# Projection of k and v of the batch after next in one block with the values of a head pair, in an attention and feed-forward kernel

## Chip, core and metric

The kernel runs on one core of a Trainium2 chip. The metric is the device time of one execution in microseconds (us). Engines are named as in the profile: PE is the matrix engine (TensorE), PEld its weight loads, DVE the vector engine, ACT the scalar engine, POOL the engine whose queue issues the input loads, SP the engine whose queue issues stores and small copies.

## What is computed

Eight batches of linear attention (keys and values of 1024 positions are projected to 64), eight heads of 64, followed by a feed-forward layer with a squared rectifier:

```python
k_proj = einsum('ks,bhsd->bhkd', E, k)          # E, F: 64 x 1024
v_proj = einsum('ks,bhsd->bhkd', F, v)
scores = q @ k_proj.T / sqrt(64)
attn   = softmax(scores, axis=-1)
x      = (attn @ v_proj)  -> rows (b, s), columns (h, d): 8192 x 512
h      = maximum(x @ w_in, 0)                   # w_in 512 x 2048
out    = (h * h) @ w_out                        # w_out 2048 x 512
```

Output is float32; the kernel computes in bf16 with float32 accumulation.

## The kernel before, in words

**Feed-forward.** A batch's tokens are two chunks of 512. Both products of the feed-forward layer are done, from batch 1 on, as block products with seven partial products in place of eight. The first product of a chunk runs in four *groups* (class `Group`), the second in `second_spread`. A generator `both()` takes one *step* at a time: one stage of a group (four matmuls of 128x256, line 680) and then one piece of the second product of the chunk before (line 594). A group takes seven steps, in the order of `F_STEPS`: p1, p5, p4 of the group before, p6, p2, p3, p7. A chunk takes 28 steps, a batch 56.

**Banks.** [...] `psum` holds four single banks (`bank0` to `bank3`) for the first product and a pair (`att_psum`) for attention; `second_pool` holds two for the second product. In a group, `first` is bank base+1, `other` is base+2, and `chain` is base+3 for an even group and base+4 (the same as base+0) for an odd one. After p2 a group has no more use for `first`, and the chain bank of the other parity is free from p4 to the next p1. Values of a head pair can therefore be computed into these two banks between p3 and the next p1: `values_lent`. DVE then has to empty them (`scale`, line 421, two instructions of 128x512) before the next group's p1 writes `first` (line 707) and ACT copies `first` to `chain` (line 708).

**Attention of the next batches** is put between the steps by a plan: `on(step, b, name, ...)` calls a method of `atts[b]` after that step. For loop index b the count starts at t = 56(b-1)+28, the middle of batch b's first products. In the 28 steps after t the attention of batch b+1 is finished; then follow the projection, transposes and scores of b+2. The methods are

- `scores(pr)`: two matmuls (line 339), exponentials on ACT (line 353), `att_psum`
- `sums_spread(pr)`: sums of two pairs (eight matmuls of 64x32 tiles, line 392), logarithm and exponential on ACT (lines 396, 397), then six SP copies that spread the inverse sums `rs` (line 403); `rs` has three buffers
- `values_products` / `scale`: four matmuls of 64x64 tiles (line 413) and the two DVE multiplications by `rs` into xT (line 421)
- `project`: sixteen matmuls, k and v in turn in tiles of 128x64 (lines 270, 271) into `att_psum`, then k twice into `kp` on DVE (lines 258, 259) and v into `vp` once on ACT (line 263) and once on DVE (line 264)
- `transpose_q_dma`, `transpose_k_dma`: SP transposes (lines 331, 304)
- `load_q`, `load_kv`: POOL loads, each held behind a named earlier instruction: `load_q` behind the last instruction that `atts[b+1].done` names when the plan reaches it, `load_kv` behind the transpose of k

**Order.** PE runs in the order written. On DVE, ACT and SP a scheduler fixes the order when the program is built, and each engine then runs its own list in order. One rule ties DVE to a lent bank: after a `values_lent`, the `relu_sum` of that group's p7 (line 697) is placed after its `scale`. In `Group`, p3 and p7 end in a `relu_sum` on DVE, p2 and p4 in a rectifier on ACT (line 690); in odd groups DVE then squares h (128x1024) and forms four sums (`sum_h`), all line 154.

Of the kernel before, what the change touches and what calls it, by code (L numbers as in the profile page):

```python
# [19 lines left out]
def kernel(  # L20
# [46 lines left out]
    turn = {"att": 0, "bank": 0, "step": 1, "pairs": 2}  # L67

    lent = ctx.enter_context(ExitStack())
# [5 lines left out]
    def att_psum(shape=(P, 2, TCH), dtype=F32):  # L75
        turn["att"] += 1
        return pair_psum(turn["att"] % turn["pairs"], shape, dtype)

    def bank(shape=(P, 512), dtype=F32, n=None):
        if n is None:  # L80
            turn["bank"] += turn["step"]
            n = turn["bank"]
        return psum.tile(list(shape), dtype, tag=f"bank{n % 4}", name="ps_bank")
# [48 lines left out]
    for j, (lo, hi) in enumerate(W_IN_PIECES):  # L132
        t = wpool.tile([P, NCB, (hi - lo) * P], BF16, name=f"w_in_{lo}")
# [7 lines left out]
    for j in range(WP):  # L141
        t = wpool.tile([P, fn, DM], BF16, name=f"w_out_{j}")
# [89 lines left out]
    class Attention:  # L232
# [170 lines left out]
                            nc.sync.dma_start(rs[j][to:to + 32], rs[0][have:have + 32])  # L403
                self.rs[pr + j] = rs[j]

        def values_products(self, pr, lent):
            ps_x = [bank(n=turn["bank"] + n)[:] for n in (1, 4)] if lent else None
            if not lent:
                ps = att_psum()
                ps_x = [ps[:, par] for par in range(2)]  # L410
            e = self.e.pop(pr)
            for o, par, a, r in VALUE_QUADS:
                nc.tensor.matmul(  # L413
                    ps_x[par][o], lhsT=self.vp[r, 2 * pr + a, :], rhs=e[r, a], start=True, stop=True
                )
            self.ps_x[pr] = ps_x
# [8 lines left out]
            return self.done  # L425

        def values(self, pr):
            self.values_products(pr, False)
            self.scale(pr)

        def values_lent(self, pr):
            self.values_products(pr, True)
            turn["lent"] = self.scale(pr)


# [303 lines left out]
    with tc.manual_schedule(engines={PE}):  # L739
# [33 lines left out]
        def at(step, fn, *args, **kwargs):  # L773
            plan.setdefault(step, []).append(lambda: fn(*args, **kwargs))
# [110 lines left out]
        def on(step, b, name, *args):  # L885
            at(step, lambda: getattr(atts[b], name)(*args))
# [5 lines left out]
        for b in range(B - 1):  # L892
            t = 56 * (b - 1) + 28
            if b:
                on(t + 1, b + 1, "scores", 3)
                on(t + 6, b + 1, "sums_spread", 2)
                on(t + 6, b + 1, "values_lent", 1)
                on(t + 10, b + 1, "values", 0)
                on(t + 20, b + 1, "values_lent", 2)
                on(t + 20, b + 1, "values_products", 3, False)  # L900
                on(t + 21, b + 1, "scale", 3)
                at(t + 24, lambda b=b: chunk[b + 1, 0].sum_x())
            at(t + 51, lambda b=b: chunk[b + 1, 1].sum_x())
            if b + 2 < B:
                if b:
                    on(t + 11, b + 2, "load_q", lambda b=b: atts[b + 1].done)
                on(t + (26 if b else 32), b + 2, "transpose_q_dma")
                on(t + (28 if b else 36), b + 2, "project")
                on(t + (30 if b else 37), b + 2, "transpose_k_dma")
                if b + 3 < B:  # L910
                    at(t + (32 if b else 37), begin, b + 3)
                    on(t + (32 if b else 37), b + 3, "load_kv", lambda b=b: atts[b + 2].kT_done)
                on(t + (44 if b else 45), b + 2, "scores", 0)
                on(t + (47 if b else 48), b + 2, "scores", 1)
                on(t + (50 if b else 51), b + 2, "sums_spread", 0)
                on(t + (53 if b else 54), b + 2, "scores", 2)
# [34 lines left out]
```

## Time and profile before

| | us |
|---|---|
| three runs | 471.1, 471.76, 474.29; median 471.76 |
| the profiled execution | 472.65, of which the span from first to last instruction is 470.9 |
| PE busy | 464.3 (99%), 4141 matmuls |
| PEld busy | 369.2 (78%) |
| DVE busy | 347.1 (74%), 596 instructions |
| ACT busy | 298.3 (63%) |
| POOL busy | 34.2 (7%) |
| granted PE clock | 0.996 |
| DMA | 64.75 MB, mean 138 GB/s |

Busy shares are means over the whole span; matmuls overlap in the pipe, so a busy PE is not one at its peak. A timeline row gives the start in us from the beginning of the span, the duration, engine, line, operation, output<-input, shape and how many equal instructions follow each other; in square brackets stands the idle time ahead of it and what ended that.

### The profile page before, as it was taken

What the parts mean: (1) busy time and instruction counts of PE and PEld (TensorE: products, weight loads), DVE (VectorE), ACT (ScalarE), POOL (GpSimd) and SP (SyncE); (2) the same over time, 40 slices, a digit from 0 to 9 for tenths busy, and PEclk for the clock granted to TensorE, in tenths of its full rate; (3) what the DMA queues carried; (4) which work ended last, traced back from release to release, by engine and by line L of the source; (5) the groups of instructions that cost most, each with busy time, mean ns of one, the idle gap of its engine ahead of it and who ended that gap; (6) DMA issues with size and microseconds to landing.
All of it is one profiled execution on the core that took longest, in us unless ns stands there. A gap on an engine that the chain in (4) does not pass through costs nothing.

```text
span 470.9 us, 10084 instructions
## 1 busy us (share of the span) xinstructions
PE 464.3 (99%) x4141; PEld 369.2 (78%) x4141; DVE 347.1 (74%) x596; ACT 298.3 (63%) x484; POOL 34.2 (7%) x47
## 2 busy tenths in 40 slices
PE   7999999999999999999999999999999999999997
PEld 3544587788888887888888888888878888888886
DVE  2468976776977779677895679777796778968571
ACT  3568777777556873688556775568736885565641
POOL 7340010100010000100001000100000000000000
PEclk8999999999999999999999999999999999999999
DMA  9999999795949577594868749495682042101012
GB/s 182 201 205 207 158 161 198 161 217 158 170 102 183 153 135 179 103 173 127 163 169 141 163 132 163 114 194 138 135 180 69 27 126 74 68 24 68 24 70 89
DMA packets 84592, 64.75 MB, mean 138 GB/s; under 512 B 33985, under 2 KB 81857, under 8 KB 84545
## 3 DMA queue, kind: packets, MB, share of 16 engines
q0 software_dynamic: 32208, 29.23, 40.4%
q1 hardware_dynamic: 52336, 34.88, 27.6%
q8 instruction: 32, 0.52, 0.5%
q14 instruction: 16, 0.12, 0.1%
HBM read 59.24 MB, written 16.78 MB: 161 GB/s over the span
## 4 chain that ended last, share of the span: by engine, by line
PE 96%; DMA 1%; ACT 1%; DVE 0%; SPq 0%; issue 0%; DVEq 0%
PE ps_bank L680 37%; PE ps_second L594 36%; PE ps_bank L513 6%; PE ps_bank L573 3%; PE ps_att L339 3%; PE ps_att L270 3%; PE ps_second L573 1%; DMA k_f<-in_k_dram 1%; PE ps_bank L413 1%; PE ps_att L392 1%; PE ps_att L413 1%; PE ps_bank L220 1%; PE ps_bank L314 1%; ACT rs L358 1%; PE ps_bank L278 1%; PE ps_att L349 0%
## 5 line engine op out<-in xcount | busy, mean ns | idle before, releaser
L154 DVE TENSOR_TENSOR h<-h 128x1024 bf16<-128x1024 bf16 (+1 forms) x170 | 105.4, 645 | 43.8 <-ACT h L690 38.6
L680 PEld LDWEIGHTS <-w_in_sum 128*128 128x128 bf16 x896 | 85.4, 98 | 20.0 <-issue 7.4
L680 PE MATMUL ps_bank<-x_sum,w_in_sum 128*128 128x256 bf16 x672 | 101.1, 273 | 0.0
L594 PEld LDWEIGHTS <-h 128*128 128x128 bf16 x896 | 87.7, 98 | 10.3
L697 DVE CUSTOM_DVE_ANT_0 h<-ps_bank,u 128x512 bf16<-128x512 f32 x112 | 74.2, 685 | 14.0 <-PE ps_bank L680 9.7
L708 ACT COPY ps_bank<-ps_bank 128x512 f32<-128x512 f32 x56 | 32.0, 571 | 82.7 <-PE ps_bank L680 82.4
L568 ACT COPY u<-ps_bank 128x512 f32<-128x512 f32 x115 | 68.0, 591 | 22.6 <-PE ps_bank L680 20.9
L690 ACT ACTIVATE h<-ps_bank 128x512 bf16<-128x512 f32 x112 | 67.9, 606 | 14.0 <-PE ps_bank L680 13.1
L680 PEld LDWEIGHTS <-w_in 128*128 128x128 bf16 x672 | 65.3, 98 | 12.1 <-issue 2.5
L594 PEld LDWEIGHTS <-s 128*128 128x128 bf16 x672 | 65.7, 98 | 7.7
L680 PE MATMUL ps_bank<-xT,w_in 128*128 128x256 bf16 x448 | 67.3, 273 | 0.0
L594 PE MATMUL ps_second<-w_out_sum,s 128*128 128x256 bf16 x448 | 67.2, 273 | 0.0
L594 PE MATMUL ps_second<-w_out_sum,h 128*128 128x256 bf16 x448 | 67.0, 273 | 0.0
L594 PE MATMUL ps_second<-w_out,h 128*128 128x256 bf16 x448 | 64.7, 272 | 0.0
L353 ACT ACTIVATE expT<-ps_att 128x1024 bf16<-128x1024 f32 x32 | 33.1, 1034 | 5.6 <-PE ps_att L339 5.3
L154 DVE TENSOR_TENSOR o_sb<-ps_second,u 128x512 f32<-128x512 f32 x29 | 19.8, 684 | 19.3 <-PE ps_second L594 13.6
L680 PE MATMUL ps_bank<-xT,w_in_sum 128*128 128x256 bf16 x224 | 33.6, 273 | 0.0
L680 PE MATMUL ps_bank<-x_sum,w_in 128*128 128x256 bf16 x224 | 33.6, 273 | 0.0
L594 PE MATMUL ps_second<-w_out,s 128*128 128x256 bf16 x224 | 33.6, 273 | 0.0
L513 PE MATMUL ps_bank<-xT,w_in 128*128 128x512 bf16 x128 | 29.1, 379 | 0.0
L421 DVE TENSOR_TENSOR xT<-ps_att,rs 128x512 bf16<-128x512 f32 x24 | 15.4, 682 | 14.9 <-PE ps_att L413 14.9
L568 ACT COPY u<-ps_second 128x512 f32<-128x512 f32 x30 | 17.6, 585 | 11.6 <-PE ps_second L594 9.3
(98 smaller groups left out, 478.7 us busy)
## 6 DMA issues: line engine op xcount, KB each, us to landing
out_dram<-o_sb SPq DMA_DIRECT2D x63, 256.0 KB, 2.4
rs<-rs SPq DMA_DIRECT2D x72, 128.0 KB, 2.3
K_sb<-in_k_dram POOLq DMA_DIRECT2D x7, 1024.0 KB, 10.0
V_sb<-in_v_dram POOLq DMA_DIRECT2D x7, 1024.0 KB, 14.6
Q_sb<-in_q_dram POOLq DMA_DIRECT2D x6, 1024.0 KB, 9.2
w_out<-in_moe_w_out_dram POOLq DMA_DIRECT2D x4, 512.0 KB, 16.3
Q_sb<-in_q_dram POOLq DMA_DIRECT2D x4, 256.0 KB, 11.0
V_sb<-in_v_dram POOLq DMA_DIRECT2D x2, 512.0 KB, 10.7
```

The source lines that it names most:

```text
L154: return nc.vector.tensor_tensor(out=o, in0=x, in1=y, op=op)
L270: nc.tensor.matmul(ps[LO, 0], lhsT=ET[:, i, :], rhs=self.K[:, :, i, :], start=f, stop=l)
L353: self.done = nc.scalar.activation(e[:], ps[:], AF.Exp, scale=SCALE)
L421: self.done = nc.vector.tensor_tensor(out=self.xT[:, pr, :, par], in0=ps_x[par].rearrange("p (c t) -> p c t", c=2), in1=rs[:, par].rearran ...
L513: nc.tensor.matmul(ps[:], lhsT=w_in_blk(cb, fb), rhs=self.xT[:, cb, self.c].rearrange("p a t -> p (a t)"), start=(cb == 0), stop=(cb == NC ...
L568: nc.scalar.copy(u[:], ps)
L573: nc.tensor.matmul(ps[:, i * HM:(i + 1) * HM], lhsT=self.h_form(n, fb)[:, i * P:(i + 1) * P], rhs=w_out_form(n, fb), start=fresh and fb == ...
L594: nc.tensor.matmul(ps[:, i * HM:(i + 1) * HM], lhsT=self.h_form(n, fb)[:, i * P:(i + 1) * P], rhs=w_out_form(n, fb), start=fresh and i == ...
L680: nc.tensor.matmul(ps[:, j * HC:(j + 1) * HC], lhsT=w_in_form(n, cb, 2 * self.g + j), rhs=self.chunk.x_form(n, cb), start=fresh and j == 0 ...
L690: nc.scalar.activation(self.out(kh, a), ps[:], AF.Relu)
L697: nc.vector._custom_dve(TENSOR_ADD_SAT, out=self.out(kh, a), in0=ps[:], in1=more[:], s0=3.0e38, s1=0.0)
L708: nc.scalar.copy(self.chain[:], self.first[:])
```

## The change

For loop index b of 1 and above, the values of pair 0 are no longer computed at step t+10 into `att_psum` but at t+13 into lent banks, after p3 of the second group (an odd one, hence the other chain bank: the argument `group`). The projection of batch b+2 (b from 1 to 5) is no longer called at t+28 but at t+13 too, right after these values, into `att_psum`. The other calls keep their steps.

```diff
-        def values_products(self, pr, lent):
-            ps_x = [bank(n=turn["bank"] + n)[:] for n in (1, 4)] if lent else None
+        def values_products(self, pr, lent=0):
+            ps_x = [bank(n=turn["bank"] + n)[:] for n in (1, 4 - lent % 2)] if lent else None
...
         def values(self, pr):
-            self.values_products(pr, False)
+            self.values_products(pr)
             self.scale(pr)
 
-        def values_lent(self, pr):
-            self.values_products(pr, True)
+        def values_lent(self, pr, group):
+            self.values_products(pr, 2 + group)
             turn["lent"] = self.scale(pr)
...
                 on(t + 1, b + 1, "scores", 3)
                 on(t + 6, b + 1, "sums_spread", 2)
-                on(t + 6, b + 1, "values_lent", 1)
-                on(t + 10, b + 1, "values", 0)
-                on(t + 20, b + 1, "values_lent", 2)
-                on(t + 20, b + 1, "values_products", 3, False)
+                on(t + 6, b + 1, "values_lent", 1, 0)
+                on(t + 13, b + 1, "values_lent", 0, 1)
+                on(t + 20, b + 1, "values_lent", 2, 2)
+                on(t + 20, b + 1, "values_products", 3)
                 on(t + 21, b + 1, "scale", 3)
...
                 if b:
                     on(t + 11, b + 2, "load_q", lambda b=b: atts[b + 1].done)
                 on(t + (26 if b else 32), b + 2, "transpose_q_dma")
-                on(t + (28 if b else 36), b + 2, "project")
+                on(t + (13 if b else 36), b + 2, "project")
                 on(t + (30 if b else 37), b + 2, "transpose_k_dma")
```

## The prediction, made before the changed kernel ran

> **What bounds the kernel now.** I read busy shares first, then what PE waited for, then the chain of waits through one batch, then the timelines of PE, DVE and ACT around the moved steps. The busy line and the waits of PE (engine, line, waited for: us, times, longest):
>
> ```profile
> PE 464.3 (99%) x4141; PEld 369.2 (78%) x4141; DVE 347.1 (74%) x596; ACT 298.3 (63%) x484; POOL 34.2 (7%) x47
> ```
>
> ```profile
> PE ps_bank L220 <- DVE zeros L123: 1.2, 1, 1.2
> PE ps_bank L278 <- ACT K_sb L742: 1.0, 1, 1.0
> PE ps_bank L211 <- DVE e_bf L741: 0.7, 1, 0.7
> PE ps_att L339 <- DVE kT L301: 0.2, 1, 0.2
> ```
>
> These four are all, and all belong to the start-up: from 95 to 400 us PE waits for nothing. Its order sets the end, so a change gains only by making PE's own list cheaper, and loses whatever new wait it puts there. What the list costs is in the chain, here in batch 2 (start, length, what):
>
> ```profile
> 164.10 0.34 PE ps_att L392 x8
> 164.44 0.34 PE ps_bank L413 x4
> 164.78 0.54 PE ps_bank L680 x4
> ...
> 168.81 0.34 PE ps_att L413 x4
> 169.15 0.54 PE ps_bank L680 x4
> 169.70 0.44 PE ps_second L594 x4
> ...
> 177.99 0.34 PE ps_bank L413 x4
> 178.33 0.22 PE ps_att L413 x4
> 178.55 0.54 PE ps_bank L680 x4
> ```
>
> Four 128x256 matmuls cost 0.44, but 0.54 straight after a block in smaller tiles; four quads cost 0.22 after quads of the same tile, 0.34 after another tile size. So entering a block costs 0.12 and leaving it 0.10. Sums and then values (64x32, then 64x64) pay the 0.12 twice. `project` enters with 0.33 where its next seven pairs take 0.21 each.
>
> The second resource is DVE, idle 2.5 us ahead of the values of pair 0 and then almost never (start, length):
>
> ```profile
> 169.21 1.29 DVE L421 TENSOR_TENSOR xT<-ps_att,rs 128x512 bf16<-128x512 f32 x2 [2.48 <-PE ps_att L413]
> 171.24 0.69 DVE L154 TENSOR_TENSOR h<-h 128x1024 bf16<-128x1024 bf16 x1 [0.74 <-ACT h L690]
> 171.84 1.28 DVE L697 CUSTOM_DVE_ANT_0 h<-ps_bank,u 128x512 bf16<-128x512 f32 x2
> ...
> 177.80 0.68 DVE L697 CUSTOM_DVE_ANT_0 h<-ps_bank,u 128x512 bf16<-128x512 f32 x1
> 178.40 1.28 DVE L421 TENSOR_TENSOR xT<-ps_bank,rs 128x512 bf16<-128x512 f32 x2
> ```
>
> See that the scale of pair 2 starts at 178.40, its first half ends 178.40+0.68 = 179.08, and p1 of the fourth group, which overwrites that lent bank, starts at 179.37 (PE timeline): a margin of 0.29.
>
> **The Trainium skill.** "TensorEngine Tiling (Array Packing)", Key Properties: changing the tiling mode drains the engine, changing only the tile does not. The trace agrees: 0.12 and 0.10 at each change, 0.22 quads within a mode. "PSUM — Partial Sum Buffer", PSUM bank collisions: the hardware doesn't arbitrate between engines on a bank, semaphores must; hence p1's wait for `scale`. No delay from it shows before. "DMA: Bandwidth & Descriptors", Issuing engines are not separate DMA queues: loads from POOL and copies from SP share 16 engines; used for the loads below. The 128x512 multiplications from PSUM take 0.68 here, which I use instead of any page's price.
>
> **The change on PE.** No matmul is added or removed (the built PE lists have equal length); places change. Removed per batch (b = 1 to 5): the lone values block at t+10, 0.34+0.10 = 0.44, and the lone project block at t+28, 0.33+7x0.21+0.10 = 1.90 with rounding. Added: one block with both. It saves one exit, 0.10, surely. Whether it saves an entry too depends on 64x64 to 128x64: sums to values, the nearest row, pays 0.12 again. I take **-0.10 a batch**, other end -0.22. For b = 6 only the values move: 0.
>
> **The change on DVE.** This is the cost. Moved into the busy stretch at t+13: two scales, two copies to kp, one to vp: five instructions. The built order there is: square, relu_sum p3, scale, square, scale, kp, kp, relu_sum p7, vp, square, sum, square, three sums, then relu_sum p3 and the scale of pair 2 in the next group. From the first square to that scale are 16 starts. Before, ten starts from 171.84 to 178.40 took 6.56, less 0.21 idle: 0.635 each; independent ones come every 0.60, dependent ones every 0.72. Take x = 0 at the start of p3 of the second group (170.84 before). The square, released by ACT, stays at x = 171.24-170.84 = 0.40. Then relu_sum 1.01, scale 1.61 (values are out of PE at 1.4), square 2.21, scale 2.82, kp 3.42 (project, begun near 1.26, ends 1.92 later as before, 3.2), kp 4.02 to 4.70, relu_sum p7 4.62 to 5.30. ACT's vp copy waits for the second kp as in the old lists, so 4.72 to 5.30; DVE's vp 5.35, square 5.95, sum 6.67, square 7.28 (it reads ACT's rectifier of p4, out near 7.0), sums 7.89, 8.50, 9.22, relu_sum p3 9.83, scale of pair 2 at 10.43, first half done **11.11**.
>
> PE on the same clock: p3 and second product to 0.88, values 0.97, project near 1.26, p7 near 3.1. After p7, spacing as before: p4 at +2.62 (six stages of 0.437) = 5.7, p1 of the fourth group at +(179.37-171.72) = 7.65, so **10.75**. DVE is late by 11.11-10.75 = 0.36, with release 0.4. Bounds: at 0.60 a start it is in time, 0; at 0.66, 0.9. I take **+0.4 a batch**. Queued behind the waiting p1 is all of PE, so it adds in full. Then ACT's copy to chain, and p4 behind it, come with that p1; nothing else is late: p4 of the second group needs relu_sum p7 by 5.7 and gets it at 5.30.
>
> ACT: its vp copy now stands ahead of the third group's chain copy (line 708). That copy could start at p1's end, 3.1+0.87+0.60 = 4.6, and starts at 5.3; p6, which needs it, comes at p7+3.5 = 6.6. Covered; without the 0.7 to spare it would add here. At t+28 DVE and ACT lose the same copies, and PE the 1.90 that hid them; DVE there was not waited for, so nothing.
>
> For b = 6 there is no project between values and p1: scale done at 1.61+0.68 = 2.29, p1 at about 2.2: **+0.1** once (0 to 0.4).
>
> **DMA and queues.** `load_q` at t+11 reads `done`, which was the scale of pair 0 (ends 170.5) and is now that of pair 1 (166.1): the 1 MB load starts 4.4 earlier, beside the six `rs` copies (issued 166.65 to 171.4, landing 2.3 median, 4.6 worst). They are needed by pair 2 at 178 or later: over 6 us of cover; nothing. On SP the k transpose now stands ahead of three stores instead of behind them; kp is there at 4.7, so it follows the q transpose directly (4.07+1.25 of SP issue). Stores wait a little; o_sb has three buffers: nothing. POOL's list is unchanged; the k and v load, held by the k transpose, comes some 10 us earlier (193.8 before), away from the next `rs` copies. k and v of b+2 for the earlier project were issued at 139.9 and 140.7 and land 10 to 15 later, against 171: 16 us of cover. The `rs` buffer of pair 3 is that of pair 1, scaled earlier as before.
>
> **Sum.** 5 x (-0.10+0.4) + 0.1 = +1.6; ends 5 x (-0.22) = -1.1 and 5 x (-0.10+0.9)+0.4 = +4.4. On the profiled execution: 472.65+1.6 = 474.3. That run is 0.89 above the median, 471.76, on which my time stands: 471.76+1.6 = **473.4**.
>
> **Rivals.** (A) DVE keeps up, the tile changes saved are all there is: 471.76 less 0.5 to 1.1, **471.0**. For it: 0.29 of margin before and a 0.60 start spacing. Against: five more instructions before the same deadline. (B) Slower by over 1%: DVE falls behind further, at the place named, p1 of the fourth group, and from 0.4 more at p4 of the second too. At 0.69 a start (the full length of an instruction, no overlap) the scale begins at 0.40+16x0.69 = 11.44, ends 12.1, wait 1.4 a batch: 5 x 1.3 + 0.4 = +6.9, **478.7**. It decides from a wait of about 1.0. Against: 0.635 was measured in this very stretch. (C) `rs` copies held up by the earlier load until it lands, 166.2+9.2 = 175.4, and one round after: 178, still in time; if each batch lost 1 us, 476.3. (D) It does nothing: saved 0.1 and a wait of 0.1 cancel, 471.8, inside A's neighbourhood.
>
> **Numbers.** Small wait as summed 0.55 (own range 471.8 to 476.2), A with D 0.28, B 0.12, C 0.05. The range, **470.6 to 476.8**, leaves out B and the tails. Within 1% means 467.0 to 476.5, about what a measurement of this kernel can tell from no change: the leading case and A lie in it, so 0.84; slower 0.13; faster 0.03, since no path offers PE 4.7 us.
>
> **What would show it.** The fused block: quads 0.34, first project pair 0.33 (0.22 if no entry is paid), exit 0.10, nothing tiled at t+28. PE's waits: about 0.4 five times on DVE's line 421 at p1 of the fourth group. If that row is missing, A holds and the DVE step is wrong; if it stands at 1 or more, or p4 appears beside it, B. PE waiting on line 403 copies would make it C.

## The result

The changed kernel takes 474.96 us, median of six runs (474.74 to 475.4), against 472.0 for six of the kernel before (470.22 to 474.29). The ratio is 1.0065, with a 95% interval from 1.0038 to 1.0092: 0.65% slower, 3.1 us of 472. The profiled execution took 474.77, its span 473.0.

The profile after, first what PE waited for from 95 to 400 us (engine, line, waited for: us, times, longest). Before, this view had no row at all:

```profile
PE ps_bank L680 <- DVE xT L421: 2.4, 5, 0.8
```

It is the row that the prediction named: p1 waits for the scale, once in each of the five batches with a projection. The shares of the engines in the chain of work that ended last, followed back from the last instruction, move the same way:

```profile
PE 87%; DVE 9%; issue 1%; ACT 1%; DMA 1%; DVEq 0%
```

Before, PE had 96% and DVE 0%. The timeline of PE shows the block and the place of the wait in batch 2 (start, length, what):

```profile
170.96 0.41 PE L413 MATMUL ps_bank<-expT,vp 64*64 64x512 bf16 x4
171.30 0.40 PE L270 MATMUL ps_att<-K_sb,ET 128*64 128x512 bf16 x1
...
173.15 0.61 PE L680 MATMUL ps_bank<-x_sum,w_in_sum 128*128 128x256 bf16 x4
...
180.38 0.60 PE L594 MATMUL ps_second<-w_out_sum,h 128*128 128x256 bf16 x4
181.38 0.60 PE L680 MATMUL ps_bank<-xT,w_in 128*128 128x256 bf16 x4 [0.41 <-DVE xT L421]
```

Before, the same two groups stood 0.44 apart:

```profile
178.93 0.60 PE L594 MATMUL ps_second<-w_out_sum,h 128*128 128x256 bf16 x4
179.37 0.60 PE L680 MATMUL ps_bank<-xT,w_in 128*128 128x256 bf16 x4
```

Starts of four-matmul groups stand 0.437 apart where nothing is in the way; in the changed kernel these are 181.38-180.38 = 1.00 apart, so PE loses 0.56. (The bracket says 0.41 because it counts from the modelled end of the pipelined matmuls; below, losses are excess over 0.437.) In batches 1 to 5 the excess is 0.57, 0.56, 0.58, 0.95 and 0.57. DVE in the same stretch of the changed kernel:

```profile
170.39 0.69 DVE L154 TENSOR_TENSOR h<-h 128x1024 bf16<-128x1024 bf16 x1 [4.07 <-ACT h L690]
171.00 0.68 DVE L697 CUSTOM_DVE_ANT_0 h<-ps_bank,u 128x512 bf16<-128x512 f32 x1
...
173.40 0.67 DVE L258 CAST kp<-ps_att 64x512 bf16<-64x512 f32 x1
174.08 0.68 DVE L259 CAST kp<-ps_att 64x512 bf16<-64x512 f32 x1
174.79 0.69 DVE L697 CUSTOM_DVE_ANT_0 h<-ps_bank,u 128x512 bf16<-128x512 f32 x1
175.52 0.69 DVE L264 CAST vp<-ps_att 64x512 bf16<-64x512 f32 x1
...
180.65 1.28 DVE L421 TENSOR_TENSOR xT<-ps_bank,rs 128x512 bf16<-128x512 f32 x2
```

DVE idles 4.07 ahead of the stretch and then never more than 0.10 until the scale of pair 2, whose first half ends at 181.34. PE starts 0.04 later. The idle time that the values at t+10 used to fill is now longer, and their work stands in the queue that was full.

Profiled executions differ in the start-up (the first sums begin between 96.4 and 99.2 us), so the kernels are best compared by the **batch period**: from the start of one batch's first sums (line 392) to that of the next batch's, in the timelines of PE. The **stage** in the table runs over all six batches: from the group of four matmuls ahead of the first such sums (98.06 in the trace of before) to a group near the end of the second layer (453.81).

| kernel | the last four periods, us | stage, us | median of the runs, us |
|---|---|---|---|
| before | 54.95 54.95 54.96 54.95 | 355.75 | 472.0 beside the changed kernel, 471.86 beside the next four, 471.04 beside the last three |
| changed | 55.41 55.42 55.79 55.42 | 358.73 | 474.96 |
| values alone | 55.41 55.69 55.65 55.56 | 358.98 | 474.49 |
| projection alone | 55.43 55.44 55.78 55.40 | 358.47 | 474.66 |
| q load later | 55.42 56.76 56.29 55.42 | 360.63 | 476.13 |
| v copies on ACT | 54.95 54.95 54.96 54.95 | 356.04 | 473.27 |
| v copies on DVE | 56.13 56.14 56.13 56.13 | 361.94 | 478.12 |
| k and v copies on ACT | 54.85 54.84 54.85 54.85 | 355.50 | 471.58 |
| the same, batch 6 as before | 54.85 54.84 54.85 54.85 | 355.21 | 471.4 |

(For before: 207.63-152.68 = 54.95 and so on. The kernels are those of the experiments below.)

### The profile page after: what moved, and what is told of

Read it like the earlier page. It is cut to its first block, busy times and chain, and to the rows that moved or that the text cites. A ratio compares the mean times of both kernels' runs of the same rounds, so it can differ in the third digit from the quotient of the medians.

```text
span 473.0 us, 10067 instructions
## 1 busy us (share of the span) xinstructions
PE 463.8 (98%) x4123; PEld 369.0 (78%) x4141; DVE 345.8 (73%) x596; ACT 298.2 (63%) x484; POOL 34.0 (7%) x47
## 4 chain that ended last, share of the span: by engine, by line
PE 87%; DVE 9%; issue 1%; ACT 1%; DMA 1%; DVEq 0%
PE ps_bank L680 34%; PE ps_second L594 33%; PE ps_bank L513 6%; PE ps_bank L573 4%; PE ps_att L339 2%; DVE h L154 2%; DVE s L154 2%; DVE h L697 2%; DVE xT L421 2%; PE ps_second L573 1%; PE ps_att L270 1%; PE ps_bank L220 1%; PE ps_att L392 1%; DMA e_f<-in_E_dram 1%; PE ps_bank L413 1%
## 5 line engine op out<-in xcount | busy, mean ns | idle before, releaser
L154 DVE TENSOR_TENSOR s<-h 128x1024 bf16<-128x1024 bf16 x32 | 22.0, 691 | 3.2 <-PE ps_second L594 1.5
```

The costliest lines, as they stand in the source:

```text
L154: return nc.vector.tensor_tensor(out=o, in0=x, in1=y, op=op)
```

## The experiments

The theory: DVE's list between p2 of the second group and the end of the chunk is full; what is moved into it makes the scale of pair 2 late, and p1 of the fourth group with it. Rivals: the `rs` copies are late, because the load of q starts earlier; or the moved values alone, or the projection alone, are to blame.

**Values alone.** Only the project call goes back.

```diff
-                on(t + (13 if b else 36), b + 2, "project")
+                on(t + (28 if b else 36), b + 2, "project")
```

> Values of pair 0 in lent banks at t+13 as in the changed kernel, project back at t+28. Theory (DVE's copies of the projection are the added work that makes the scale of pair 2 late): no saved tile change, and per batch only the small waits that batch 6 shows in the changed kernel, 0.14 and 0.10 in six batches, +1.5 against before, 473.5 us. Rival (the load of q, released earlier, holds up the rs copies): that load stays early here, so the wait of 0.57 stays at p1 of the fourth group in every batch, +3.4, 475.4 us. Rival (moving the values is what costs): as the changed kernel or above, 475.

Measured: 474.49 (ratio 1.0072, 1.0052 to 1.0092), more than the 473.5 expected and less than either rival. PE's excess is 0.14 at p1 of the third group in all six batches, 0.10 to 0.40 at p1 of the fourth, and 0.18 early in the next chunk in five. There a product of the second layer waits for ACT's copy out of its bank (line 610); that copy stands behind ACT's copy to vp, which waited for DVE's second copy to kp:

```profile
133.80 0.58 ACT L263 CAST vp<-ps_att 64x512 bf16<-64x512 f32 x1 [0.21 <-DVE kp L259]
135.37 0.61 ACT L610 COPY ps_second<-ps_second 128x512 f32<-128x512 f32 x1
136.03 1.03 PE L594 MATMUL ps_second<-w_out,h 128*128 128x256 bf16 x8
```

These sum to 0.86+1.37+0.9 = 3.1; the stage is 3.23 longer. So two scales taken out of DVE's idle time cost as much as the whole change (2.98), spread over three places, and the rival that moving the values is what costs is borne out in size; batch 6 of the changed kernel, my source for the 0.25, has no projection behind it, so it could not show the third place. And in two batches DVE really waited for `rs`:

```profile
232.02 0.68 DVE L697 CUSTOM_DVE_ANT_0 h<-ps_bank,u 128x512 bf16<-128x512 f32 x1
232.90 1.29 DVE L421 TENSOR_TENSOR xT<-ps_bank,rs 128x512 bf16<-128x512 f32 x2 [0.20 <-DMA rs<-rs]
```

The rival about the load is thus no fiction: here DVE waits up to 0.2 for the copies where it comes early enough to notice.

**Projection alone.** Only the values go back to the attention pair.

```diff
-                on(t + 13, b + 1, "values_lent", 0, 1)
+                on(t + 10, b + 1, "values", 0)
```

> Projection at t+13 as in the changed kernel, values of pair 0 back at t+10 in the attention pair. Theory (DVE's copies of the projection): the chain from the second copy to kp on is the same and starts when PE is done with project; PE pays a block of its own (no 0.10 saved) and p1 of the fourth group waits about 0.46 in five batches, +2.3 against before, 474.3 us. Rival (the early load of q): the load is behind the scale of pair 0 again as before, so no wait, 472.0 us. Rival (the scales moved are what costs): no wait either, 472.0 us.

Measured: 474.66 (1.0078, 1.0057 to 1.01), as the theory had it (474.3). The excess at p1 of the fourth group is 0.48 in three batches, 0.83 and 0.46 in two, and there is no other. The load of q is behind the scale of pair 0 here, so it isn't the cause. Either half of the change fills DVE's list enough, and the costs don't add up: the stage is 2.72 longer with the projection alone, 3.23 with the values alone and 2.98 with both. With the projection alone DVE stands idle ahead of its first copy, until PE has finished the projection:

```profile
174.35 0.68 DVE L258 CAST kp<-ps_att 64x512 bf16<-64x512 f32 x1 [0.54 <-PE ps_att L271]
```

In the changed kernel the two scales fill that time, so they lengthen the wait only from 0.48 to 0.57. Nor is there a wait at p1 of the third group, where batch 6 and the values alone lose 0.14: the projection stands between the values and that p1.

**The q load later.** Same kernel, the load held behind the scale of pair 0 again.

```diff
-                    on(t + 11, b + 2, "load_q", lambda b=b: atts[b + 1].done)
+                    on(t + 14, b + 2, "load_q", lambda b=b: atts[b + 1].done)
```

> The changed kernel with the load of q planned at t+14, so that it is held behind the scale of pair 0, as before. Theory (DVE): nothing changes but where the load lies; p1 of the fourth group waits 0.57 five times, 475.0 us. The rs copies go back to landing in 2.3 us. Rival (rs copies held up by the load): the waits go, only the saved tile changes are left, 471.5 us.

Measured: 476.13 (1.0099, 1.0075 to 1.0123), with the waits of PE:

```profile
PE ps_bank L680 <- DVE xT L421: 2.4, 5, 0.8
PE ps_bank L680 <- ACT u L568: 1.4, 2, 1.1
```

The first row is that of the changed kernel to the digit, although the median `rs` copy lands in 2.3 us as before, not 2.6, and the longest in 4.6, not 7.6. The rival falls. The second row is new and was in nobody's expectation. On SP the q transpose now waits until 241.20 for the later load (in the changed kernel it starts at 233.11 in this batch), the stores come behind it, and ACT stands still until one of them has landed and frees an output buffer:

```profile
241.20 4.32 SPq L331 DMA_TRANSPOSE qT<-Q_sb  x1
245.57 9.54 SPq L588 DMA_DIRECT2D out_dram<-o_sb  x4
```

```profile
254.13 0.58 ACT L584 COPY o_sb<-ps_second 128x512 f32<-128x512 f32 x1 [2.78 <-DMA out_dram<-o_sb]
```

So the earlier load in the changed kernel is needed: it keeps the q transpose, which stands ahead of these stores, from holding them up.

**Both v copies on ACT.** One DVE instruction less in the stretch.

```diff
-            nc.vector.tensor_copy(self.vp[LO], view)
+            nc.scalar.copy(self.vp[LO], view)
```

> The changed kernel with both copies to vp on ACT, which idles about 3 us there; one DVE instruction of some 0.7 us less between project and the scale of pair 2, one ACT instruction of 0.58 more. Theory (DVE backlog): the wait of 0.57 shrinks to 0 to 0.1, the saved tile changes are left, 0.5 below before but for 0.25 in batch 6: 471.8 us. Rival (rs copies, or anything off DVE): 475.0 us as the changed kernel. If ACT's chain copy (line 708) comes too late for p6, a PE wait on line 708 appears.

Measured: 473.27 (1.003, 1.0016 to 1.0043); PE waits for nothing from 95 to 400 us, and the period is back at 54.95. About 0.09 of excess is left at p1 of the fourth group (the first half of the scale ends at 179.97, p1 starts at 180.02), which eats the saved tile change. The time is 1.5 above the 471.8 expected. In the trace 0.93 of this lies in the start-up: the edit reaches the two projections there as well, and PE shows 0.50 of excess at 59.4 us and 0.43 at 90.2, which no other run has. The rest fits the stage, 0.29 longer than before where 0.25 less was expected.

**Both v copies on DVE.** One more in the stretch.

```diff
-            nc.scalar.copy(self.vp[HI], view)
+            nc.vector.tensor_copy(self.vp[HI], view)
```

> The changed kernel with both copies to vp on DVE: one DVE instruction of about 0.65 us more between project and the scale of pair 2. Theory (DVE backlog): the wait at p1 of the fourth group goes from 0.57 to 1.2 in five batches, in part as a wait at p4 of the second group, whose relu_sum comes 1.3 later than its 0.4 of margin allows; batch period from 55.4 to about 56.1, 478 us in all. Rival (nothing of DVE decides any more, PE's own list does): 475.

Measured: 478.12 (1.0147, 1.0127 to 1.0168). The wait has moved to where the theory said that a longer backlog would bite first, p4 of the second group behind the relu_sum of p7:

```profile
176.52 0.60 PE L594 MATMUL ps_second<-w_out_sum,s 128*128 128x256 bf16 x4
178.15 0.60 PE L680 MATMUL ps_bank<-x_sum,w_in 128*128 128x256 bf16 x4 [1.03 <-DVE h L697]
```

These starts are 1.63 apart, an excess of 1.19; at p1 of the fourth group only 0.10 is left, as PE is late already. The stage is 6.19 longer than before; what is left of the 7.1 between the medians lies outside it. Against the changed kernel, one DVE instruction less or more behind the projection changes the period by -0.47 and +0.71.

**k and v copies on ACT.** Three of the four copies of the moved projection on ACT, the start-up's projections left alone.

```diff
-        def project(self):
+        def project(self, second=nc.vector.tensor_copy, other=nc.vector.tensor_copy):
...
-            self.keep_k(ps[LO, 0], slice(0, H))
-            self.keep_v(ps[HI, 1])
+            self.keep_k(ps[LO, 0], slice(0, H), second)
+            self.keep_v(ps[HI, 1], other)
...
+                on(t + (13 if b else 36), b + 2, "project", *([nc.scalar.copy] * 2 if b else []))
```

(In `keep_v`, `other` takes the place of DVE's copy.)

> The changed kernel with three of the four copies of the moved projection on ACT (second to kp, both to vp), from the call at t+13 on, so that the start-up stays as it is. Theory (DVE backlog): the wait at p1 of the fourth group is gone in batches 1 to 5 and the saved tile change of 0.10 shows by itself: period 54.85 instead of 54.95 before; batch 6 keeps 0.25. In all 0.3 below before: 471.6 us, same within the measurement. Rival (ACT becomes late: its chain copy waits for three copies, p6 then for it): a PE wait on line 708 in each batch, period above 54.95.

Measured: 471.58 (1.0002, 0.9987 to 1.0016). PE doesn't wait in batches 1 to 5, on DVE or on ACT; the period is 54.85. Here and in the next run the saved tile change stands by itself: 0.10 a batch.

**The same, batch 6 as before.**

```diff
-                on(t + 13, b + 1, "values_lent", 0, 1)
+                if b + 2 < B:
+                    on(t + 13, b + 1, "values_lent", 0, 1)
+                else:
+                    on(t + 10, b + 1, "values", 0)
```

> As the run with three copies on ACT, and the values of pair 0 of the last batch, which has no projection beside it, back at t+10 in the attention pair. Theory: the two waits of batch 6 (0.14 and 0.10) go as well, 0.5 below before in all: 471.4 us, the fastest of the kernels here by its trace, though hardly to be told from before by the times. Rival (ACT late): as in that run.

Measured: 471.4 (1.0001, 0.9985 to 1.0016). The stage is 355.21 long against 355.75: 0.54 less, as summed. By the times it is the same as before.

## Why the prediction was right

**Direction, place and order of size: right.** The prediction said 473.4 in a range from 470.6 to 476.8; 474.96 came, +3.0 where it summed +1.6: the size is a little over half, and the terms below say where the rest was. Its likeliest case happened, at the row named, in all five batches.

**PE's list: right.** The entry from values to project is paid (0.34 for the quads, as the row of sums and values had it), one exit is saved: -0.10, shown by 54.85 against 54.95.

**DVE's row of starts: right in its order, 0.23 short in its length.** From the first square to the scale of pair 2 the sum had 10.03, the trace has 180.65-170.39 = 10.26. Most of the shortfall lies at the second copy to kp: it starts 0.68 after the first, and the next instruction 0.71 after it, where the sum took 0.60 both times. The wait for ACT ahead of vp, 0.73, was as summed. The mean start that the prediction had measured before, 0.635, times sixteen is 10.16 and would have come nearer than its sum of single steps. PE was 0.07 later than summed. Wait predicted 0.4, measured 0.57.

**Terms that were too small.** Of the 1.38 that the sum was short, five times 0.17 is 0.85, 0.38 one batch and 0.15 batch 6. One batch shows 0.38 more than the others: DVE sits idle for 0.47 ahead of a sum at 288.12, and the profile names a matmul. It is there in batch 4 of this run, and about as much more stands in batch 4 of the projection alone and of the later load, not in the others; why is open, and it was no term of the prediction. Batch 6 pays 0.14 at p1 of the third group, where 0.1 was summed, and 0.10 more at the fourth, which was not. So 5 x (-0.10+0.57)+0.38+0.25 = 2.98, and the stage measured 358.73-355.75 = 2.98.

**ACT: right.** Its vp copy waits 3.20 for the second kp and starts its chain copy at 175.46, ahead of p6 at 176.66; no PE wait on line 708. With both v copies on ACT little of that was left: the chain copy ends at 175.73 and p6 starts at 175.78, and still no such wait came.

**DMA: right that nothing waits in the changed kernel, wrong on the cover.** The prediction left six microseconds between the issue of the last `rs` copy and its reader. With the load beside them the first five copies took 8.48 us to issue, not 3.46. Before and after:

```profile
166.65 3.46 SPq L403 DMA_DIRECT2D rs<-rs  x5
166.25 8.48 SPq L403 DMA_DIRECT2D rs<-rs  x5
```

The last was issued at 175.56 and landed at 178.34, 2.3 us before the scale. Part of that margin is the projection's own time on PE, which now stands ahead of the scale: with k and v copies on ACT, where DVE isn't late, the last copy still landed at 176.74 for a scale at 177.95; with values alone, without that time, DVE waited for `rs` twice.

**Rivals.** A (a clean gain of 0.5) did not happen in the changed kernel; it is what the copies on ACT make of it, in the stage. B's mechanism, the wait at p4, exists and begins with one more DVE instruction; the wait of 1.0 from which it decides was not reached. C is refuted by the later load. The saved 0.1 and the wait don't cancel, so D is out.

## What to carry to other kernels

When PE never waits, price a move by the engine that empties PE's banks: write down its built order with start-to-start times and compare with PE's next use of each bank. A block put together to save PE tile changes saved 0.10 a batch, and the five vector instructions that came with it into a full queue cost 0.57. Where in the queue they stand matters more than their number: two scales ahead of the point where DVE would have waited for PE anyway made 0.09 of that, one copy behind it 0.48. With no projection behind them the same two scales cost 3.23 over the six batches. Share such copies out to the engine that idles there before moving them, and check what else is released by the moved instruction: here a load.

## What the runs showed of the hardware

A copy from PSUM on 64 partitions takes DVE as long as a multiplication on 128 (0.67 to 0.69 for 512 elements). In the changed kernel the second copy to kp, from one half of the partitions to the other, starts 0.68 after the first copy and the next instruction 0.71 after it, not 0.60; with that copy moved to ACT, the next instruction follows the first copy by 0.60. The first five of six small SP copies beside a 1 MB load from POOL took 8.5 us to issue where they took 3.5 without it. In both, in batch 2, the fifth was issued 0.05 to 0.06 after the second had landed and the sixth as soon after the fourth, so the later issue goes with slower landings (up to 7.4 us for the first four, where it was 2.3); what makes the issue wait is not shown.
